# Alpha turned on TensorE, a third half-tile buffer, shared weight scales and a new issue table

## The chip, the cores and the metric

The kernel runs on one core of a Trainium2 chip, in one launch. The metric is the device time of that core in microseconds. One execution was recorded by the hardware profiler; the times on all the tables below are microseconds from the start of that recording unless marked ns.

## The reference

Attention with a learned relative bias, followed by a two-layer feed-forward part. Batch 4, 8 heads, sequence 576, head size 64; 2,304 tokens of width 512, hidden width 2,048.

```python
scores = q @ k.T / 8
x = log1p(abs(i - j)) / log1p(max(i, 1))        # one number per (i, j)
bias = relu(x * w1 + b1) @ w2                   # 32 hidden values -> 8 heads
attn = softmax(scores + bias) @ v               # all in float32
h = attn_rows @ w_in                            # 2304 x 512 @ 512 x 2048
g = max(h, 0) + alpha * min(h, 0)               # alpha: one per hidden column
out = g @ w_out                                 # 2304 x 2048 @ 2048 x 512
```

The two weight matrices arrive as 64-bit floats and are taken apart on the chip with integer operations.

## The kernel before

The kernel keeps near-full precision by splitting most operands into two 16-bit halves, a high and a low one, and adding three matmuls of them. To split a tensor it needs its largest absolute value: one reduction over the columns, a transposition on TensorE, a reduction of the row, a matmul that spreads the result over all partitions (`allmax`, L453 to L461), and four small VectorE operations that make a power of two of it (`p2`, L443 to L452).

The stages are these.
- **Constants and alpha** (L410 to L442). A table of logarithms `cst` is loaded and scaled in place on VectorE by values made of w1 and b1 (L426, L427). `alpha` is loaded by L420 as a 128 x 16 tile, one number at a time. Two half-tile buffers `a16` are cleared at L409.
- **Bias tiles** (`bias_tile`, 36 of them). Each takes four rectified rows from the table on ScalarE (L479), VectorE (L476) or GpSimd (L482), multiplies them by w2 on TensorE (L497), takes the result out of PSUM (L507, L508) and writes it to a scratch area in DRAM, from which the attention units read it back skewed.
- **Weights** (`weights`, L651 to L699), eight blocks of 256 hidden columns. Each block is loaded, put together from 64-bit floats on VectorE (L667, L670), its maxima of w_in and w_out are taken (L674 to L678), the scales made, and the two halves written (high on ScalarE or GpSimd, L691, L692, L697, L698; low on VectorE, L386).
- **q, k and v** (`qk_turn`, `v_rows`). Rows are loaded and turned on TensorE (L577); for v only the maximum is needed (L391, through `absmax`) and, for batches 1 to 3, the halves (L629, L630).
- **Attention units** (`unit`), 8 per batch. Scores (L602 or L603), bias added with the row minimum of the negated sum (L799), exponential (L802), reciprocal of the row sum (L805, L807). For batch 0 the rows are normalised (L822, L823), turned on TensorE (L831) and multiplied with v (L860). For batches 1 to 3 they are normalised into two 16-bit halves in an `a16` buffer (L812 or L813 for the high half, L815 for the low one), turned by a transposing DMA (L818) and multiplied with v by L852. The result goes as halves into a chunk of x (L878, L880).
- **MLP chunks** (`chunk`, `layer_pair`), nine of 256 tokens. For each weight block: first layer L930, activation L937 and L938, halves L941 to L943, second layer L949, output L911, L912, L915.

The order is not left to a scheduler. Every operation has a number, in the order in which the program creates it, and three tables fix the rest: ISSUE lists all 2,806 numbers in the order of issue (a suffix such as .1 picks the second of the engines that may do it), SLOT gives each buffer its place, and IDLE puts dummy matmuls (L997) ahead of certain operations on TensorE: 118 in all. Each engine executes its own operations in the order of the table, waiting where an input is missing; all transfers but a few at the start are issued on SP's queue.

Of the kernel before, what the change touches and what calls it, by code (L numbers as in the profile page):

```python
# [9 lines left out]
F32 = mybir.dt.float32  # L10
# [9 lines left out]
P = 128  # L20
# [122 lines left out]
"""  # L143
IDLE = """
20:11 115:2 52:6 73:2 108:1 35:5 59:3 680:3 94:2 213:2 189:5 45:5 66:1 244:1 631:3 947:2 949:2 652:2 129:1 624:3 687:2 150:2 136:2 708:4 715:2 505:1
694:3 701:5 511:1 743:1 729:5 376:3 542:3 573:7 761:1 775:1 411:2 796:7 786:2 818:2
"""

# [901 lines left out]
```

## Time and profile before

| | us |
|---|---|
| median of 3 runs | 705.16 |
| lowest and highest | 702.3, 707.93 |
| the profiled execution | 702.73 |
| its span | 700.9 |
| TensorE busy | 667.7 (95%) |
| VectorE busy | 498.4 (71%) |
| ScalarE busy | 402.7 (57%) |
| GpSimd busy | 174.7 (25%) |

The span goes from the first to the last instruction that the profiler saw; 1.83 us of the profiled execution lie around it. PE is TensorE, DVE VectorE, ACT ScalarE, POOL GpSimd, SP SyncE; PEld is TensorE's weight load, which overlaps its matmuls. "Busy" counts the time in which the engine executes something; a busy share over the whole span mixes stages with different limits. TensorE's granted clock was full (0.999 on the mean).

### The profile page before, as it was taken

How to read it: one execution, taken by the hardware profiler on the slowest of the kernel's cores; microseconds unless marked ns; L12 is line 12 of the kernel's file. 1: busy time of each engine (PE TensorE's matmuls, PEld its weight loads, DVE VectorE, ACT ScalarE, POOL GpSimd, SP SyncE). 2: the span in 40 equal slices, each digit the busy share in tenths (PEclk: the TensorE clock that was granted, in tenths of full speed). 3: DMA queues.
4: the chain of work that ended last, by engine and by line, in shares of the span. 5: the costliest groups of instructions: out<-in, count | busy, mean ns of one | idle time of the engine just before them, and what ended most of it. 6: DMA issues, size and time to landing. Idle time of an engine off the chain costs nothing.

```text
span 700.9 us, 15311 instructions
## 1 busy us (share of the span) xinstructions
PE 667.7 (95%) x5739; PEld 423.2 (60%) x5739; DVE 498.4 (71%) x1227; ACT 402.7 (57%) x822; POOL 174.7 (25%) x233
## 2 busy tenths in 40 slices
PE   7898899989999999999999999999999999999997
PEld 3454445556656566665667666667566567666664
DVE  5899999997788698987866866677667555232422
ACT  4788999877765575644656465555645352122212
POOL 2555123342113123132322321210221311101010
PEclk9999999999999999999999999999999999999999
DMA  8999899777589799999999979897969963200100
GB/s 199 276 287 340 308 297 297 250 191 189 152 186 182 182 201 221 187 207 220 217 212 179 190 170 205 157 212 172 230 134 196 182 149 62 38 31 1 45 1 31
DMA packets 236374, 125.89 MB, mean 180 GB/s; under 512 B 204684, under 2 KB 204684, under 8 KB 236300
## 3 DMA queue, kind: packets, MB, share of 16 engines
q1 hardware_dynamic: 236168, 124.91, 76.5%
q8 instruction: 45, 0.74, 0.4%
q14 instruction: 29, 0.24, 0.1%
q10 hardware_dynamic: 132, 0.00, 0.0%
HBM read 73.88 MB, written 15.61 MB: 128 GB/s over the span
## 4 chain that ended last, share of the span: by engine, by line
PE 67%; DVE 10%; ACT 9%; DMA 7%; issue 4%; POOL 1%; ACTq 0%; SPq 0%; DVEq 0%; POOLq 0%
PE H L930 24%; PE O L949 22%; PE S L603 5%; PE A L852 5%; DMA at<-a 4%; DVE fg L799 2%; PE S L497 2%; PE S L577 2%; ACT fg L507 2%; PE O L497 2%; ACT at L479 2%; DVE a L815 2%; DMA x<-in_moe_w_out_dram 1%; ACT fg L802 1%; PE A L860 1%
## 5 line engine op out<-in xcount | busy, mean ns | idle before, releaser
L930 PE MATMUL H<-x,win 128*128 128x256 f16 x1728 | 200.7, 273 | 1.5 <-DVE mg L938 1.5
L949 PE MATMUL O<-wout,mg 128*128 128x512 f16 x864 | 197.3, 379 | 1.1 <-DVE mg L915 0.7
L930 PEld LDWEIGHTS <-win 128*128 128x128 f16 x1728 | 166.3, 98 | 34.1 <-issue 8.3
L937 ACT ACTIVATE mg<-H,sm 128x256 f32<-128x256 f32 x144 | 63.6, 469 | 136.8 <-PE H L930 121.1
L949 PEld LDWEIGHTS <-mg 128*128 128x128 f16 x864 | 83.0, 98 | 93.1 <-issue 3.3
L938 DVE SCALAR_TENSOR_TENSOR mg<-H,sm,mg 128x256 f32<-128x256 f32 x144 | 65.4, 478 | 97.8 <-ACT mg L937 97.8
L802 ACT ACTIVATE fg<-fg,st 128x576 f32<-128x576 f32 x144 | 110.5, 768 | 32.3 <-DVE st L799 28.8
L815 DVE SCALAR_TENSOR_TENSOR a<-fg,st,a 128x576 f16<-128x576 f32 x108 | 91.8, 853 | 35.8 <-POOL a L812 17.7
L799 DVE CUSTOM_DVE_ANT_0 fg<-S,fg 128x576 f32<-128x576 f32 x127 | 93.6, 749 | 14.8 <-PE S L603 11.1
L812 POOL TENSOR_SCALAR a<-fg,st 128x576 f16<-128x576 f32 x59 | 47.7, 808 | 179.1 <-DMA at<-a 114.5
L943 POOL TENSOR_TENSOR mg<-mg 128x512 f16<-128x512 f32 x37 | 46.2, 1252 | 120.0 <-DVE mg L941 54.4
L603 PE MATMUL S<-qk 64*128 64x288 f16 (+1 forms) x684 | 55.0, 284 | 5.0 <-DVE qk L584 2.9
L852 PE MATMUL A<-at,five 128*64 128x256 f16 (+3 forms) x720 | 51.5, 288 | 0.6 <-DVE x L880 0.6
L603 PEld LDWEIGHTS <-qk 64*128 64x128 f16 (+1 forms) x720 | 34.2, 96 | 24.7 <-issue 19.1
L813 ACT ACTIVATE a<-fg,st 128x576 f16<-128x576 f32 x49 | 37.6, 770 | 17.3 <-DMA at<-a 15.3
L852 PEld LDWEIGHTS <-five 128*64 128x64 f16 (+1 forms) x720 | 36.1, 109 | 15.2 <-issue 12.0
L805 POOL TENSOR_SCALAR st<-st 128x2 f32<-128x2 f32 (+1 forms) x41 | 12.7, 309 | 105.2 <-ACT fg L802 101.4
L497 PE MATMUL S<-at,w2b 128*32 128x79 f32 (+38 forms) x432 | 34.2, 334 | 4.7 <-ACT fg L507 2.0
L482 POOL TENSOR_SCALAR at<-cst,npsi 128x320 f32<-128x320 f32 (+14 forms) x34 | 27.7, 819 | 44.2 <-PE S L497 25.6
L479 ACT ACTIVATE at<-cst 128x528 f32<-128x528 f32 (+16 forms) x51 | 32.6, 665 | 10.4 <-DVE cst L426 4.2
L997 PE MATMUL H<-sm 128*128 128x512 f16 x118 | 34.8, 406 | 0.9 <-DVE sm L413 0.9
L941 ACT ACTIVATE mg<-mg 128x512 f16<-128x512 f32 x36 | 22.6, 627 | 22.7 <-DVE mg L938 16.6
(150 smaller groups left out, 856.4 us busy)
## 6 DMA issues: line engine op xcount, KB each, us to landing
fg<-scr SPq DMA_DIRECT2D x64, 576.0 KB, 4.7
scr<-fg SPq DMA_DIRECT2D x36, 295.5 KB, 5.1
x<-in_moe_w_out_dram SPq DMA_DIRECT2D x13, 512.0 KB, 5.2
fg<-scr SPq DMA_DIRECT2D x32, 144.0 KB, 3.4
out_dram<-mg SPq DMA_DIRECT2D x18, 256.0 KB, 2.7
five<-in_q_dram SPq DMA_DIRECT2D x32, 128.0 KB, 3.8
mg<-in_moe_w_in_dram SPq DMA_DIRECT2D x8, 512.0 KB, 5.7
x<-in_moe_w_in_dram SPq DMA_DIRECT2D x8, 512.0 KB, 5.5
```

The source lines that it names most:

```text
L479: nc.scalar.activation(hb.t[:, 0:wd], R[:, 0:wd], AF.Relu, bias=PSI[:, g:g + 1], scale=1.0)
L497: nc.tensor.matmul(ps.t[32 * gl:32 * gl + 32, c:n], lhsT=w2b, rhs=x, start=True, stop=True)
L603: return [(lambda a, dst=dst, zq=zq, zk=zk, i=i: nc.tensor.matmul(dst(a), lhsT=tr16(qt)[at, 0, pr, zq, lo:lo + n], rhs=tr16(qt)[at, 1, pr, ...
L799: V(lambda x=x, sl=sl, st=st, ls=ls: nc.vector.tensor_tensor_reduce(out=in_halves(ls[x]()), in0=halves(sl[x].t), in1=in_halves(ls[x]()), s ...
L802: A(lambda x=x, st=st, ls=ls: nc.scalar.activation(ls[x](), ls[x](), AF.Exp, bias=st.t[:, x:x + 1], scale=-1.0, accum_out=st.t[:, 2 + x:3 ...
L812: pl.op([("POOL", 775, lambda x=x, rec=rec, ls=ls, a16=a16: nc.gpsimd.tensor_scalar(a16.t[:, 0:S], ls[x](), rec(), 1.0, op0=ALU.mult, op1= ...
L815: V(lambda x=x, rec=rec, ls=ls, a16=a16: nc.vector.scalar_tensor_tensor(a16.t[:, 640:640 + S], ls[x](), rec(), a16.t[:, 0:S], op0=ALU.mult ...
L852: nc.tensor.matmul(ps.t[64 * hh:64 * hh + 64, 0:w], lhsT=v5[0:hi, zv, n, 2 * pr + hh, :], rhs=at16(at)[0:hi, 5 * za + n, 320 * hh:320 * hh ...
L930: nc.tensor.matmul(hb.t[:, f, :], lhsT=win[:, fp, zw, kb, P * f:P * f + P], rhs=x[:, zx, kb, :], start=(n == 0), stop=(n == 11))
L937: A(lambda f=f: nc.scalar.activation(gf(f), hb.t[:, f, :], AF.Copy, scale=cu[:, f:f + 1]), 470, ky, [hb, t_sig], [(g, f)])
L938: V(lambda f=f: nc.vector.scalar_tensor_tensor(gf(f), hb.t[:, f, :], cs[:, f:f + 1], gf(f), op0=ALU.mult, op1=ALU.max), 475, ky, [hb, t_si ...
L949: nc.tensor.matmul(ob.t[:, t, :], lhsT=gg.t[:, zg, f, P * t:P * t + P], rhs=wout[:, fp, zw, f, :], start=(first and f == 0 and (zg, zw) == ...
```

## The change

Alpha is loaded as 16 rows of 128 numbers, turned by TensorE into PSUM and copied out by VectorE; the transposition is the first operation in TensorE's order, behind twelve dummies. The two `a16` buffers are cleared behind the batch-0 attention units instead of at the start, and a third one lies over the first 640 columns of the constants, cleared when the last bias tile has read them. The weight blocks 0 and 1, and 2 and 3, share one `allmax` and one `p2` of four columns. The maximum of v of batch 0 may go to ScalarE. ISSUE, SLOT and IDLE are replaced throughout: 2,793 operations, 112 dummy matmuls in 39 places.

```diff
-694:3 701:5 511:1 743:1 729:5 376:3 542:3 573:7 761:1 775:1 411:2 796:7 786:2 818:2
+678:2 685:6 727:2 713:2 506:3 706:2 526:5 741:3 557:2 327:1 395:1 780:1 802:5
...
     c_a16 = slots("a16", 2, [P, 1280], F16)
+    c_a16.tiles.append(cstt[:, 0:640].bitcast(F16))
+    c_a16.units.append({("a16", 2)})
...
-    t_gap = [["gap"] for _ in range(2)]
-    for a in range(2):
-        V(lambda a=a: nc.vector.memset(c_a16.tiles[a], 0.0), 700, KEY0 + 900, w=[t_gap[a]])
+    t_gap = [["gap"] for _ in range(3)]
...
-    DMA(lambda e: e.dma_start(out=al, in_=alpha.rearrange("(c p) -> p c", p=P)), 8192, KEY0 + 500, w=[t_al], act_q=True)
+    alr = sb.tile([P, P], F32, name="alr")
+    t_alr = ["alr"]
+    DMA(lambda e: e.dma_start(out=alr[0:16], in_=alpha.rearrange("(c p) -> c p", p=P)), 0, KEY0 + 500, w=[t_alr], act_q=True)
+    aps = Buf(cA)
+    PE(lambda: nc.tensor.transpose(aps.t[:, 0:16], alr[0:16], EYE[0:16, 0:16]), 270, KEY0 + 500, [t_alr, t_c], [aps])
+    V(lambda: nc.vector.tensor_copy(al, aps.t[:, 0:16]), SMALL, KEY0 + 500, [aps], [t_al])
...
-    w_tok = [["w", i] for i in range(NFP)]
+    W_PAIR = 4
+    w_tok = [["w", i - i % 2 if i < W_PAIR else i] for i in range(NFP)]
+    for i in range(0, W_PAIR, 2):
+        w_tok[i + 1] = w_tok[i]
...
-            absmax(mx[:, hf:hf + 1], s, key, [s], [(tok, hf)])
+            alts = [("DVE", 1476, lambda hf=hf, s=s: nc.vector.tensor_reduce(mx[:, hf:hf + 1], s.t, AX.X, ALU.max, apply_absolute_value=True))]
+            if b == 0:
+                alts.append(("ACT", 1450, lambda hf=hf, s=s: nc.scalar.activation(c_a16.tiles[hf], s.t, AF.Abs, accum_out=mx[:, hf:hf + 1])))
+            pl.op(alts, key, [s], [(tok, hf)] + ([t_gap[hf]] if b == 0 else []), tag="mv")
...
-        ar = allmax(m, 2, key, tok)
-        p, ip, s = p2(ar, 2, 2.0 ** -30, key, tok)
...
+        w_late[fp] = (a, bb, va, vb)
+        if fp < W_PAIR and fp % 2 == 0:
+            return
+        fps = [fp - 1, fp] if fp < W_PAIR else [fp]
+        nw = 2 * len(fps)
+        ar = allmax(w_mx[:, 2 * fps[0]:2 * fps[0] + nw], nw, key, tok)
+        p, ip, s = p2(ar, nw, 2.0 ** -30, key, tok)
...
+        for n, fp in enumerate(fps):
+            halves_of(fp, 2 * n, s, tok, key)
...
+    pl.begin("gap", KEY0)
+    for a in range(2):
+        V(lambda a=a: nc.vector.memset(c_a16.tiles[a], 0.0), 700, KEY0 + 900, w=[t_gap[a]])
+    V(lambda: nc.vector.memset(c_a16.tiles[2], 0.0), 700, KEY0 + 900, w=[t_gap[2], t_R, t_T])
     for b in range(1, B):
```

`halves_of` holds the splitting that stood at the end of `weights`, unchanged but for the column of the scales. What the new tables do shows in their first rows, here by engine, as the operation and its part of the program. SP: the constants, w2, alpha, two pieces of weight block 0, then nine of the ten pieces of q and k of batch 0 in a row (before: the constants, b1, a piece of q, w2, alpha, and then q, k and weight pieces mixed). ScalarE: the transfers of b1 and w1, then rectified rows; the warming exponential (L414), which was its first computation, stands behind 21 operations. VectorE: the copy of alpha and alpha's maximum stand ahead of the scaling of the table (L426). At the very end one of the last two output halves is taken out by VectorE and one by ScalarE (before: both by ScalarE).

## Rows read from the trace of the kernel before

**Rows 1.** Busy time by stretch: start:end, length, then busy us of each engine.

```profile
0.00:164.43 164.43, 146.75 (x1442) 78.25 (x1443) 147.40 (x369) 136.97 (x242) 61.21 (x86) 1.00 0.90 269
164.43:250.00 85.57, 82.69 (x668) 54.51 (x668) 68.76 (x190) 54.98 (x116) 19.68 (x31) 1.00 0.78 173
250.00:400.00 150.00, 144.16 (x1255) 95.69 (x1254) 119.64 (x292) 87.41 (x189) 44.06 (x59) 1.00 1.04 208
400.00:560.00 160.00, 158.19 (x1386) 103.95 (x1386) 110.64 (x265) 86.53 (x196) 33.71 (x43) 1.00 0.89 182
560.00:690.00 130.00, 130.00 (x969) 88.23 (x969) 49.96 (x109) 34.68 (x77) 16.04 (x16) 1.00 0.21 47
```

The busy columns are PE, PEld, DVE, ACT and POOL, each with its number of instructions; then PE's granted clock, the busy share of the DMA engines and GB/s.

**Rows 2.** The chain that ended last: start, us, what (first L930).

```profile
164.43 2.73 PE H L930 x24
```

**Rows 3.** Busy time by stretch, up to the first L930; columns as in rows 1.

```profile
0.00:20.00 20.00, 16.29 (x141) 7.16 (x141) 11.24 (x29) 9.33 (x15) 5.42 (x12) 1.00 0.88 215
20.00:60.00 40.00, 35.76 (x441) 19.38 (x439) 37.77 (x79) 32.76 (x55) 21.64 (x28) 1.00 1.02 286
60.00:130.00 70.00, 63.44 (x657) 33.72 (x656) 67.83 (x167) 68.57 (x121) 22.89 (x31) 1.00 0.93 310
130.00:164.43 34.43, 31.27 (x209) 18.00 (x208) 30.56 (x97) 26.30 (x55) 11.26 (x17) 1.00 0.72 196
```

**Rows 4.** Groups by line: busy us, mean ns of one | idle before, releasers.

```profile
L997 PE MATMUL H<-sm 128*128 128x512 f16 x118 | 34.8, 406 | 0.9 <-DVE sm L413 0.9
...
L448 DVE TENSOR_SCALAR sm<-A 128x2 f32<-128x2 f32 (+1 forms) x13 | 2.0, 152 | 0.0
L459 DVE TENSOR_REDUCE sm<-A 2x1 f32<-2x128 f32 (+1 forms) x19 | 5.2, 274 | 2.5 <-PE A L458 2.3
L391 DVE TENSOR_REDUCE sm<-five 128x1 f32<-128x1280 f32 x8 | 11.7, 1475 | 0.0
L409 DVE MEMSET a<- 128x640 uint32 x2 | 1.2, 592 | 0.2
L476 DVE TENSOR_SCALAR at<-cst 128x560 f32<-128x560 f32 (+11 forms) x21 | 10.9, 525 | 3.7 <-PE S L497 3.4 <-PE O L497 0.2
L823 DVE TENSOR_SCALAR fg<-fg,st 128x576 f32<-128x576 f32 x10 | 5.3, 527 | 0.1
L546 ACT ACTIVATE qk<-five 128x1280 f16<-128x1280 f32 x9 | 11.4, 1263 | 1.5 <-DVE sm L735 1.5
L479 ACT ACTIVATE at<-cst 128x528 f32<-128x528 f32 (+16 forms) x51 | 32.6, 665 | 10.4 <-DVE cst L426 4.2 <-PE O L497 3.5 <-PE S L497 2.6
L691 ACT ACTIVATE wout<-wout,sm 128x512 f16<-128x512 f32 x6 | 4.3, 713 | 0.0
```

**Rows 5.** Instructions in order of time, the first 8 us: start, us, engine, line.

```profile
1.18 0.73 SPq L417 DMA_DIRECT2D sm<-in_b_dram  x1
...
1.90 1.28 ACT L414 ACT_TABLE_LOAD   x1 [1.90 <-issue]
...
3.08 0.47 SPq L420 DMA_DIRECT2D sm<-in_moe_alpha_dram  x1
...
3.59 2.98 SPq L524 DMA_DIRECT2D five<-in_q_dram  x1
...
6.18 0.16 DVE L425 TENSOR_TENSOR sm<-sm 128x1 f32<-128x1 f32 x1 [0.65 <-DMA sm<-in_b_dram]
...
7.01 0.52 DVE L426 TENSOR_SCALAR cst<-cst,sm 128x576 f32<-128x576 f32 x1
```

**Rows 6.** Who waited for whom: engine, line, cause: us in total, times, longest.

```profile
POOL a L812 <- DMA at<-a: 114.5, 35, 12.6
...
ACT a L813 <- DMA at<-a: 15.3, 16, 3.0
...
PE A L852 <- DVE x L880: 0.6, 1, 0.6
```

**Rows 7.** Instructions in order of time, the end, on ScalarE.

```profile
696.33 1.27 ACT L911 ACTIVATE mg<-O,sm 128x512 f32<-128x512 f32 x2 [4.81 <-PE O L949]
```

More of the change, by code (lines that the diff above doesn't have):

```diff
@@ L34 @@
 ISSUE = """
[91 rows of a table removed]
[91 rows of a table added]
 """
 SLOT = """
[15 rows of a table removed]
[15 rows of a table added]
 """
 IDLE = """
-20:11 115:2 52:6 73:2 108:1 35:5 59:3 680:3 94:2 213:2 189:5 45:5 66:1 244:1 631:3 947:2 949:2 652:2 129:1 624:3 687:2 150:2 136:2 708:4 715:2 505:1
-694:3 701:5 511:1 743:1 729:5 376:3 542:3 573:7 761:1 775:1 411:2 796:7 786:2 818:2
+7:12 442:1 444:2 73:6 115:3 108:2 52:5 80:2 59:2 664:1 94:4 170:3 45:2 87:1 629:1 122:5 650:2 622:1 636:1 129:1 671:5 481:3 643:3 136:2 692:3 699:4
+678:2 685:6 727:2 713:2 506:3 706:2 526:5 741:3 557:2 327:1 395:1 780:1 802:5
 """
@@ L635, in attention_then_moe @@
     w_mx = cols(16)
-    w_s = {}
+    w_s, w_late = {}, {}
     class Region:
@@ L675, in weights @@
                ("ACT", 1245, lambda: nc.scalar.activation(win[:, fp, 1].rearrange("p a b -> p (a b)"), a.t[:, 0:1024], AF.Abs, accum_out=m[:, 0:1]))],
-              key, [a], [(tok, 0), wreg[fp, 0]], tag="wi")
+              key, [a], [(tok, (fp, 0)), wreg[fp, 0]], tag="wi")
         A(lambda: nc.scalar.activation(wout[:, fp, 1].rearrange("p a b -> p (a b)"), bb.t[:, 0:1024], AF.Abs, accum_out=m[:, 1:2]),
-          1245, key, [bb], [(tok, 1), wreg[fp, 1]])
-        ar = allmax(m, 2, key, tok)
@@ L680, in weights @@
-        p, ip, s = p2(ar, 2, 2.0 ** -30, key, tok)
-        V(lambda: nc.vector.tensor_tensor(pr[:, fp:fp + 1], p[:, 0:1], p[:, 1:2], op=ALU.mult), SMALL, key, [tok], [(t_pr, fp)], cont=True)
-        for i, x, vw, dst in ((0, a, va, lambda z: win[:, fp, z]), (1, bb, vb, lambda z: wout[:, fp, z])):
-            sp = s[:, i:i + 1]
-            ht = ["wh", fp, i]
-            w_s[fp, i] = ht
-            if i:
-                so = cols(2)
-                V(lambda so=so, sp=sp: nc.vector.tensor_scalar(so, sgn[:, 2 * fp:2 * fp + 2], sp, None, op0=ALU.mult), SMALL, key, [tok, t_nal], [(tok, 2)], cont=True)
-                for f in range(2):
-                    sf = so[:, f:f + 1]
-                    on_act = lambda f=f, vw=vw, dst=dst, sf=sf: nc.scalar.activation(dst(0)[:, f], vw()[:, f], AF.Copy, scale=sf)
-                    on_pool = lambda f=f, vw=vw, dst=dst, sf=sf: nc.gpsimd.tensor_scalar(dst(0)[:, f], vw()[:, f], sf, 1.0, op0=ALU.mult, op1=ALU.mult)
-                    pl.op([("ACT", 700, on_act), ("POOL", 690, on_pool)], key, [x, tok], [(ht, (0, f)), wreg[fp, i]], tag="wh")
-                    LO(lambda dst=dst, f=f: dst(1)[:, f], lambda vw=vw, f=f: vw()[:, f], lambda sf=sf: sf, lambda dst=dst, f=f: dst(0)[:, f], 512, key,
-                       [x, tok, (ht, (0, f))], [(ht, (1, f)), wreg[fp, i]])
-                continue
-            on_act = lambda x=x, vw=vw, dst=dst, sp=sp: nc.scalar.activation(dst(0), vw(), AF.Copy, scale=sp)
-            on_pool = lambda vw=vw, dst=dst, sp=sp: nc.gpsimd.tensor_scalar(dst(0), vw(), sp, 1.0, op0=ALU.mult, op1=ALU.mult)
-            pl.op([("ACT", 1137, on_act), ("POOL", 1180, on_pool)], key, [x, tok], [ht, wreg[fp, i]], tag="wh")
-            LO(lambda dst=dst: dst(1), vw, lambda sp=sp: sp, lambda dst=dst: dst(0), 1024, key, [x, tok, ht], [ht, wreg[fp, i]])
@@ new lines, in weights @@
+          1245, key, [bb], [(tok, (fp, 1)), wreg[fp, 1]])
+        w_late[fp] = (a, bb, va, vb)
[5 more added lines that the diff above has]
+        p, ip, s = p2(ar, nw, 2.0 ** -30, key, tok)
+        pairs = p.rearrange("p (n two) -> p n two", two=2)
+        V(lambda: nc.vector.tensor_tensor(pr[:, fps[0]:fps[0] + len(fps)].rearrange("p (n o) -> p n o", o=1), pairs[:, :, 0:1], pairs[:, :, 1:2], op=ALU.mult), SMALL, key, [tok], [(t_pr, z) for z in fps], cont=True)
@@ new lines, in weights, with halves_of @@
+        for n, fp in enumerate(fps):
+            halves_of(fp, 2 * n, s, tok, key)
+    def halves_of(fp, c0, s, tok, key):
+        a, bb, va, vb = w_late[fp]
+        if True:
+            for i, x, vw, dst in ((0, a, va, lambda z: win[:, fp, z]), (1, bb, vb, lambda z: wout[:, fp, z])):
+                sp = s[:, c0 + i:c0 + i + 1]
+                ht = ["wh", fp, i]
+                w_s[fp, i] = ht
+                if i:
+                    so, so_t = cols(2), ["so", fp]
+                    V(lambda so=so, sp=sp: nc.vector.tensor_scalar(so, sgn[:, 2 * fp:2 * fp + 2], sp, None, op0=ALU.mult), SMALL, key, [tok, t_nal], [so_t], cont=True)
+                    for f in range(2):
+                        sf = so[:, f:f + 1]
+                        on_act = lambda f=f, vw=vw, dst=dst, sf=sf: nc.scalar.activation(dst(0)[:, f], vw()[:, f], AF.Copy, scale=sf)
+                        on_pool = lambda f=f, vw=vw, dst=dst, sf=sf: nc.gpsimd.tensor_scalar(dst(0)[:, f], vw()[:, f], sf, 1.0, op0=ALU.mult, op1=ALU.mult)
+                        pl.op([("ACT", 700, on_act), ("POOL", 690, on_pool)], key, [x, tok, so_t], [(ht, (0, f)), wreg[fp, i]], tag="wh")
+                        LO(lambda dst=dst, f=f: dst(1)[:, f], lambda vw=vw, f=f: vw()[:, f], lambda sf=sf: sf, lambda dst=dst, f=f: dst(0)[:, f], 512, key,
+                           [x, tok, so_t, (ht, (0, f))], [(ht, (1, f)), wreg[fp, i]])
+                    continue
+                on_act = lambda x=x, vw=vw, dst=dst, sp=sp: nc.scalar.activation(dst(0), vw(), AF.Copy, scale=sp)
+                on_pool = lambda vw=vw, dst=dst, sp=sp: nc.gpsimd.tensor_scalar(dst(0), vw(), sp, 1.0, op0=ALU.mult, op1=ALU.mult)
+                pl.op([("ACT", 1137, on_act), ("POOL", 1180, on_pool)], key, [x, tok], [ht, wreg[fp, i]], tag="wh")
+                LO(lambda dst=dst: dst(1), vw, lambda sp=sp: sp, lambda dst=dst: dst(0), 1024, key, [x, tok, ht], [ht, wreg[fp, i]])
```

212 rows, old and new, of tables (ISSUE, SLOT) are left out of this document.

## The prediction

> **What bounds the kernel now.** I read the table of busy time by stretch first, then the chain, then the groups, the waits and the start. The table [rows 1] has to be read with one instant in mind, 164.43 us, where the chain shows the first matmul of the MLP's first layer, L930 [rows 2]. From there TensorE is the bound: it is idle for 85.57 - 82.69 = 2.88 us up to 250, 150.00 - 144.16 = 5.84 up to 400, 160.00 - 158.19 = 1.81 up to 560 and not at all from 560 to 690. That is 10.5 us in 525, so after 164.43 a change can win 10.5 us at the most, whatever it does to the other engines.
>
> Before 164.43 nothing on TensorE counts for its own length. It is idle for 17.7 us, and 34.8 of its 146.75 busy us are the 118 dummy matmuls of L997 [rows 4], which only fill waits. VectorE is busy for 147.40 us and ScalarE for 136.97. Split up [rows 3], VectorE is idle for 8.8 us up to 20, then 2.2, 2.2 and 3.9; ScalarE for 10.7, 7.2, 1.4 and 8.1. Between 60 and 130 both are full (67.83 and 68.57 of 70). So the time is: the instant at which these two have put the weights, the bias table and the first attention units behind them, plus TensorE's work from there. The second term hardly changes; the first is what the change works on.
>
> **The change part by part.** I counted, from the two issue tables, which operations have to be issued before the first L930: its inputs, theirs, and all that stands ahead of these on their engines. On VectorE that is 329 operations before and 317 after; on ScalarE 194 and 201; on GpSimd 81 and 82; SP issues 130 and 136 transfers; the dummies are 118 and 112, all of them ahead of it. Durations are those of [rows 4].
>
> VectorE, ahead of the first L930:
> - Two pairs of weight blocks share one maximum and one set of scales. Per pair four small operations and one product (L448 to L451 and L681, each taken at the 0.152 of L448) and one reduction (L459, 0.274) go: 1.03, twice, -2.1 us.
> - One maximum of half of v for batch 0 goes to ScalarE: -1.475 (L391).
> - Two clears at the start (L409, 0.592) go, one of the three new ones lies ahead of L930 (the others come later): -0.6. The copy of the turned alpha: +0.15.
> - Four more bias rows (L476, 0.525): +2.1. Four fewer normalisations (L823, 0.527; GpSimd takes them): -2.1.
> - Six small operations on the scales come earlier, +0.9 at 0.15; five others (three clears, two additions) go, -0.75 at the same price.
>
> Sum: -3.9 us, from 147.4 to 143.5. These durations overlap their neighbours a little, so it is the upper end of what VectorE gains.
>
> ScalarE: the maximum of v (like L546, 1.263), three more bias rows (L479, 0.665 each, 2.0) and two more weight halves (L691, 0.713 each, 1.43): +4.7, from 137.0 to 141.7. GpSimd gives up seven bias rows and a weight half, and takes the four normalisations, three clears and two additions; with 61 us of 164 busy it is not on the path.
>
> So work is moved from the fuller engine to the less full one, and the sum of the two (284.4 us) stays as it is: 285.2. Neither can start before the inputs are there. With the idle time up to 20 us as the part that is not to be had, VectorE could reach 164.43 at 147.4 + 8.8 = 156.2 at the earliest and ScalarE at 137.0 + 10.7 = 147.7; after the change it is 152.3 and 152.4. The floor of the stage falls by 3.8 us. But before, 8.2 us were lost above that floor while ScalarE had room, and now both are full to the same level, so each wait of one for the other is harder to fill. If VectorE alone decides, I get -3.9; if ScalarE decides (1.4 us idle of 70 between 60 and 130), +4.7; if the sum of both does, nothing. I take **-2.0**, half of the floor's fall.
>
> A rule of the Trainium skill speaks against one detail. The row first: ScalarE loads a function table once, 1.28 us, at 1.90 us, while it has nothing to do until the table is scaled at 7.53 [rows 5], and this one load serves the whole kernel. After the change the warming exponential stands behind some 20 us of ScalarE's other work, and the first function is a rectifier. The page "ScalarE: Activation LUTs" (section "What ACT_TABLE_LOAD costs") gives about 2.66 us, with the drain, for every switch to another set, while its section on table sets says that rectifier, copy and absolute value lie in every set. If the rectifier brings a set without the exponential, a second load falls into ScalarE's full stretch: by the page an estimated 2.7 us less gain. From rows alone it is 0 or 1.28; I take 0, as the one load here does serve both kinds.
>
> Alpha. Before, a transfer of 2,048 single numbers is issued at 3.08, and the next issue on SP's queue takes 2.98 us, where the two rows ahead of it took 0.73 and 0.47 [rows 5]. As 16 rows of 512 bytes this stall of some 2.5 us should go. But in this stretch VectorE waits for b1 [rows 5] and later for TensorE's bias matmuls, not for a load behind that stall. Between nothing and -2.5, I take **-0.5**. The new transposition is the first operation in TensorE's order behind twelve dummies, and its copy stands ahead of the scaling of the table (L426, ended 7.53), for which every bias row waits. Alpha is now issued third on SP, near 1.8; b1 was issued at 1.18 and awaited until 6.18, 5.0 us. Taking as long, it lands at 6.8, and the scaling ends up to 0.8 later (0.6 for the landing and some 0.2 for the transposition and the copy, the rest lying beside other small operations); if it lands by 6.2, as b1 did, the cost is nothing. A clear of 0.6, which stood in that place on VectorE, is gone too: I take 0.
>
> The third half-tile buffer. GpSimd waits 114.5 us for transposing transfers before it may write a half again, ScalarE 15.3 [rows 6]. GpSimd has room. The 15.3 us on ScalarE hold up what is queued behind, the MLP's activations among them. But TensorE itself waits for its attention matmul on these halves (L852) once, 0.6 us, and that for something else [rows 6]. So the buffer is worth between nothing and the 10.5 us of TensorE's idle time after 164.43. I take **-1.5**, near the row of L852. What is late next are the halves of q and k and the row minima, not the transfers. The three clears cost 0.6 each on VectorE near the first L930; the table's readers are all done before the third, so nothing else waits for it.
>
> The end. Both last output halves leave PSUM on ScalarE one after the other, 1.27 us [rows 7]; the new order puts one on VectorE: **-0.6**, or nothing if both still wait for the same matmul.
>
> Removed on TensorE: two small transpositions and four tiny matmuls, and six dummies. All lie ahead of 164.43 among waits: 0.
>
> Sum: -2.0 - 0.5 - 1.5 - 0.6 = -4.6. The profiled execution took 702.73 (span 700.9 and 1.8 around it), which gives 698.1. The median shown is 705.16, 2.4 higher, by the scatter of single runs; on it the forecast is **700.6 us**.
>
> **The rivals.**
> - Larger gain (chance 0.2): VectorE was the only bound, the loads come 2.5 us sooner, and the third buffer lets two thirds of TensorE's 10.5 us of idle time go: -3.9 - 2.5 - 7.0 - 0.6 = -14.0, 691.2. For it: VectorE's 95% between 20 and 130. Against it: TensorE's waits after 164.43 name other causes.
> - No effect (0.2): the work is only exchanged between two full engines and the new order is as tight as the old: only the end gains, 704.6. It is also the case in which buffer and alpha do what they say without anything waiting for them. For it: the unchanged sum of 285 us.
> - Slower (0.15): ScalarE takes VectorE's place as the bound of the first stage. Place: 60 to 130 us. It decides from the point where more than ScalarE's 1.4 us of idle time there is added to it; 4.7 - 0.6 gives 709.3. Against it: 8.1 us of idle time behind 130 and 7.2 ahead of 60 can take some of it.
> - The forecast has 0.45, with 696 to 704 as its own range.
>
> **How the numbers follow.** About 1% (7 us) is what a measurement of this kernel can tell from no change: below 698.1 is faster, above 712.2 slower. Faster: nearly all of the large gain (0.19), a third of the forecast (0.15) and a little of the rest: 0.36. Slower: a third of the slower rival and some of the scatter, 0.07. Same: 0.57. The range reaches from the large gain, 690, to the slower rival, 710.
>
> **What would show it.** Right: the first L930 near 162; ScalarE's and VectorE's busy time up to there within 2 us of each other; no long issue behind alpha's; GpSimd's waits for the transposing transfers clearly below 114.5; TensorE's idle time from there to 560 near 9. Wrong: the first L930 later, with ScalarE full from 60 on and VectorE waiting for it, or a second table load (the slower rival); or TensorE's idle time after it halved (the large gain).

## The result, and the profile after

The median after the change is 709.09 us (20 runs, 706.25 to 712.61), before it 705.03 us (20 runs). The ratio is 1.0059, with a 95% interval from 1.0044 to 1.0075: 4.1 us slower where 4.6 us of gain were forecast. The time lies inside the stated range and below the 1% that was named as what can be told from no change, but the interval leaves no room for a gain. In the changed kernel the lines have moved: first layer L930 is L953, second layer L949 is L972, the halves L812, L813 and L815 are L835, L836 and L838, the scaling of the table L426 is L431. (Experiments 7 and 9 to 15, whose tables are printed anew, count three lines more, L956 for L953; experiments 3 and 8 count two more than the kernel before, L814 for L812.)

The profiled execution took 706.25, with a span of 704.5. The table by stretch of the changed kernel, columns as in [rows 1], cut at its own first MLP matmul:

```profile
0.00:167.20 167.20, 145.21 (x1438) 76.38 (x1438) 144.82 (x357) 140.38 (x250) 63.32 (x89) 0.99 0.89 263
167.20:250.00 82.80, 78.37 (x646) 52.62 (x644) 63.75 (x177) 53.40 (x116) 17.63 (x28) 1.00 0.79 174
250.00:400.00 150.00, 144.63 (x1256) 96.22 (x1254) 119.06 (x289) 87.26 (x189) 36.45 (x49) 1.00 1.03 204
400.00:560.00 160.00, 157.87 (x1383) 104.01 (x1383) 113.14 (x277) 85.54 (x196) 38.21 (x51) 1.00 0.92 190
```

Two losses stand there. The first MLP matmul starts at 167.20, not at 164.43. And behind it TensorE is idle for 82.80 - 78.37 = 4.43, then 5.37, then 2.13 us: 11.9 up to 560, where [rows 1] gave 10.5 for a stretch 2.8 us longer. The third buffer should have lowered that number, and GpSimd does wait less for the transposing transfers (who waited for whom, changed kernel; [rows 6] had 114.5 and 15.3):

```profile
POOL a L835 <- DMA at<-a: 67.8, 17, 12.4
ACT a L836 <- DMA at<-a: 5.3, 6, 1.7
POOL cst L835 <- DMA at<-cst: 3.4, 1, 3.4
```

The start shows a delay ahead of the first loss. Instructions in order of time, changed kernel, first 12 us (compare [rows 5]):

```profile
0.72 1.14 ACTq L417 DMA_DIRECT2D sm<-in_b_dram  x1
1.89 0.55 ACTq L416 DMA_DIRECT2D sm<-in_w_dram  x1
1.99 0.42 SPq L422 DMA_DIRECT2D alr<-in_moe_alpha_dram  x1
2.45 0.42 SPq L673 DMA_DIRECT2D x<-in_moe_w_in_dram  x1
2.92 0.47 SPq L673 DMA_DIRECT2D x<-in_moe_w_out_dram  x1
3.43 7.43 SPq L529 DMA_DIRECT2D five<-in_q_dram  x5
9.50 0.15 DVE L426 TENSOR_REDUCE sm<-sm 128x1 f32<-128x1 f32 x1 [8.64 <-DMA sm<-in_w_dram]
10.68 0.52 DVE L431 TENSOR_SCALAR cst<-cst,sm 128x576 f32<-128x576 f32 x1
```

w1, 0.5 KB, is issued at 1.89 and VectorE waits for it until 9.50, so the table is scaled at 11.20 instead of 7.53: 3.7 us later, before any bias row can start. From there to the first MLP matmul the stage takes 167.20 - 11.20 = 156.0 us, against 164.43 - 7.53 = 156.9 before. In this pair of executions the exchange between VectorE and ScalarE gained 0.9 and the start lost 3.7. One execution of each kernel does not settle such numbers: experiment 3 has the same operations up to the first MLP matmul as the kernel before, and scales its table at 7.45, yet in its profiled execution that matmul starts 2.6 us later. In order of time, TensorE, experiment 3:

```profile
167.05 2.79 PE L932 MATMUL H<-x,win 128*128 128x256 f16 x24
```

So the sizes of the losses are taken from the medians of the experiments.

### The profile page after: what moved, and what is told of

Same layout as the page of the kernel before. It is cut to its first block, busy times and chain, and to the rows that moved or that the text cites. A ratio compares the mean times of both kernels' runs of the same rounds, so it can differ in the third digit from the quotient of the medians.

```text
span 704.5 us, 15254 instructions
## 1 busy us (share of the span) xinstructions
PE 665.5 (94%) x5728; PEld 421.3 (60%) x5728; DVE 495.9 (70%) x1214; ACT 400.5 (57%) x824; POOL 173.9 (25%) x235
## 4 chain that ended last, share of the span: by engine, by line
PE 54%; DVE 5%; DMA 3%; issue 3%; ACT 2%; POOL 1%; SPq 0%; POOLq 0%; DVEq 0%; ACTq 0%
PE H L953 22%; PE O L972 21%; PE A L875 5%; PE S L611 4%; DMA at<-a 3%; PE S L585 1%; ACT fg L825 1%; DVE fg L822 1%; DVE mg L961 1%; DVE a L838 1%; ACT mg L960 1%; POOL a L835 1%; DVE mg L965 0%; DVE cst L838 0%; PE O L611 0%
## 5 line engine op out<-in xcount | busy, mean ns | idle before, releaser
L953 PE MATMUL H<-x,win 128*128 128x256 f16 x1728 | 200.8, 273 | 1.4 <-DVE mg L961 1.2
L972 PE MATMUL O<-wout,mg 128*128 128x512 f16 x864 | 197.9, 379 | 2.5 <-DVE mg L938 1.2
L953 PEld LDWEIGHTS <-win 128*128 128x128 f16 x1728 | 166.8, 98 | 35.9 <-issue 8.1
L972 PEld LDWEIGHTS <-mg 128*128 128x128 f16 x864 | 82.1, 98 | 95.5 <-issue 7.5
L838 DVE SCALAR_TENSOR_TENSOR a<-fg,st,a 128x576 f16<-128x576 f32 x74 | 64.5, 874 | 22.5 <-ACT a L836 11.2
L835 POOL TENSOR_SCALAR a<-fg,st 128x576 f16<-128x576 f32 x42 | 34.2, 816 | 118.0 <-DMA at<-a 67.8
L828 POOL TENSOR_SCALAR st<-st 128x2 f32<-128x2 f32 (+1 forms) x48 | 15.1, 315 | 114.9 <-ACT fg L825 108.7
L502 PE MATMUL S<-at,w2b 128*32 128x79 f32 (+37 forms) x492 | 36.2, 334 | 5.7 <-ACT at L484 2.5
L484 ACT ACTIVATE at<-cst 128x432 f32<-128x432 f32 (+17 forms) x53 | 32.7, 647 | 11.1 <-DVE cst L432 5.7
L845 POOL TENSOR_SCALAR fg<-fg,st 128x576 f32<-128x576 f32 x30 | 24.5, 825 | 35.8 <-PE S L610 13.6
L836 ACT ACTIVATE a<-fg,st 128x576 f16<-128x576 f32 x32 | 24.4, 768 | 12.4 <-DMA at<-a 5.3
L838 DVE SCALAR_TENSOR_TENSOR cst<-fg,st,cst 128x576 f16<-128x576 f32 x34 | 28.1, 827 | 4.3 <-ACT cst L836 4.0
```

What stands on the lines that cost most here:

```text
L502: nc.tensor.matmul(ps.t[32 * gl:32 * gl + 32, c:n], lhsT=w2b, rhs=x, start=True, stop=True)
L835: pl.op([("POOL", 775, lambda x=x, rec=rec, ls=ls, a16=a16: nc.gpsimd.tensor_scalar(a16.t[:, 0:S], ls[x](), rec(), 1.0, op0=ALU.mult, op1= ...
L838: V(lambda x=x, rec=rec, ls=ls, a16=a16: nc.vector.scalar_tensor_tensor(a16.t[:, 640:640 + S], ls[x](), rec(), a16.t[:, 0:S], op0=ALU.mult ...
L953: nc.tensor.matmul(hb.t[:, f, :], lhsT=win[:, fp, zw, kb, P * f:P * f + P], rhs=x[:, zx, kb, :], start=(n == 0), stop=(n == 11))
L972: nc.tensor.matmul(ob.t[:, t, :], lhsT=gg.t[:, zg, f, P * t:P * t + P], rhs=wout[:, fp, zw, f, :], start=(first and f == 0 and (zg, zw) == ...
```

## The experiments

All ratios are to the kernel before, with their 95% intervals. My theory at the outset: the late small transfer at the start, and a new order behind the first MLP matmul that loses what the third buffer gains.

**1. w1 first.** The two small transfers on ScalarE's queue change places (2 is w1, 3 is b1).

```diff
-0 3.1 2.1 9 10 11 13 12 5 4 6
+0 2.1 3.1 9 10 11 13 12 5 4 6
```

> The changed kernel, with w1's transfer issued ahead of b1's on ScalarE's queue (two numbers of the issue table change places). Theory (the start): VectorE waited for w1 until 9.50 us instead of 4.49, and the whole first stage is late by that. Then w1 lands near 5, the table is scaled by 8 instead of 11.2, the first L953 comes near 164 instead of 167.2, and the ratio to the kernel before falls from 1.006 to between 0.999 and 1.002. Rival (the new order packs worse, or ScalarE is the bound): the start has slack behind it, the first L953 stays within 1 us of 167, and the ratio stays above 1.004.

Measured: 1.0061 [1.0039, 1.0083]. A miss. In order of time, w1 first:

```profile
4.47 0.15 DVE L426 TENSOR_REDUCE sm<-sm 128x1 f32<-128x1 f32 x1 [3.61 <-DMA sm<-in_w_dram]
10.27 0.16 DVE L430 TENSOR_TENSOR sm<-sm 128x1 f32<-128x1 f32 x1 [5.26 <-DMA sm<-in_b_dram]
```

Now w1 is there at 4.47 and b1, issued second at 1.90, at 10.27. Which of the two goes first is all one; the second is late.

**2. The kernel before with b1 first.** The same exchange in the old kernel: b1 goes to ScalarE's queue ahead of w1.

```diff
-2 4.1 9 10 7 0 5 11 13
+2 5.1 4.1 9 10 7 0 11 13
```

> The kernel before, with b1's transfer moved from SP's queue to ScalarE's and ahead of w1's, as the changed kernel has it; nothing else changes. Theory (the place on the queue makes w1 late): w1 lands later than 7, the first L930 comes 2 to 4 us later than 164.4, ratio 1.003 to 1.006. Rival (w1 is late in the changed kernel because two weight pieces of 512 KB are issued near it, which here come at 6.6): w1 lands by 6.2, where b1 was awaited anyway, and the ratio is within 0.001 of 1.

Measured: 1.0009 [0.9996, 1.0022]. w1, again issued second (1.91), is awaited until 6.50, not 9.50, and the table is scaled at 8.94. So the second place, with its later issue (1.91 instead of 0.73), makes w1 2.0 us late; the 3 us beyond that come from something else in the changed kernel.

**3. The third buffer alone.** The kernel before, its order untouched; the half tiles take three buffers in turn, and one clear follows the first MLP operation.

```diff
     c_a16 = slots("a16", 2, [P, 1280], F16)
+    c_a16.tiles.append(cstt[:, 0:640].bitcast(F16))
+    c_a16.units.append({("a16", 2)})
```

> The kernel before with the third half-tile buffer alone: one more clear behind the first L930, the buffers taken in turn by three, the same issue order. Theory (TensorE does not wait for these buffers): GpSimd's wait for the transposing transfers falls from 114.5 us to under 70, TensorE's idle time between the first L930 and the end stays within 1.5 us of 10.9, ratio 0.999 to 1.001. Rival (the prediction's term and its larger case): TensorE's idle time falls by 1.5 to 7 us, ratio 0.990 to 0.998.

Measured: 0.9941 [0.9923, 0.9959], 4.1 us faster (0.0059 of 704): the rival of what I expected. Who waited for whom, third buffer alone:

```profile
POOL a L814 <- DMA at<-a: 23.4, 8, 11.5
POOL cst L814 <- DMA at<-cst: 13.2, 4, 6.1
```

GpSimd waits 36.6 us for the transfers, half of the 71.2 in the changed kernel, from the same three buffers. So the buffer brings more than the prediction gave it, and something in the changed kernel takes that away.

**4. w1 first, alpha as single numbers.** Experiment 1 with alpha loaded again as 2,048 single numbers, from the same place in SP's order; the transposition turns a constant instead, with the same instructions.

```diff
-    DMA(lambda e: e.dma_start(out=alr[0:16], in_=alpha.rearrange("(c p) -> c p", p=P)), 0, ...
+    DMA(lambda e: e.dma_start(out=al, in_=alpha.rearrange("(c p) -> p c", p=P)), 8192, ...
```

> As e1_w1_first, with alpha loaded as 2,048 single numbers again; the transposition and the copy stay, on the identity and into an unused place. Theory (alpha's form stalls nothing, since the changed kernel has the long issues behind it all the same): ratio within 0.0015 of that of e1_w1_first. Rival (the prediction: the stall of 2.5 us belongs to the single numbers): the issues behind alpha take 2 to 3 us more in all and the ratio is 0.002 to 0.004 above that of e1_w1_first.

Measured: 1.0023 [1.0010, 1.0036]. The slow form of alpha is the faster one, by 0.4%, which neither expectation had. In order of time, alpha as single numbers:

```profile
2.46 2.57 SPq L673 DMA_DIRECT2D x<-in_moe_w_in_dram  x1
5.07 0.47 SPq L673 DMA_DIRECT2D x<-in_moe_w_out_dram  x1
5.58 4.16 SPq L529 DMA_DIRECT2D five<-in_q_dram  x5
6.33 0.16 DVE L430 TENSOR_TENSOR sm<-sm 128x1 f32<-128x1 f32 x1 [1.38 <-DMA sm<-in_b_dram]
```

The stall behind alpha is back (2.57 us for an issue that took 0.42), and it holds the second 512 KB piece back until 5.07. b1 lands by 6.33. Without the stall both pieces, 1 MB, are issued by 3.4 us, and b1's 0.5 KB is there only at 10.27 (experiment 1), about when that megabyte is. The stall also costs SP nothing in the end: the five pieces of q are issued by 5.58 + 4.16 = 9.74, in the changed kernel by 3.43 + 7.43 = 10.86.

**5. The weight pieces held.** The changed kernel with w1 first; the two weight pieces (193 and 205), and the operations that read them, go behind five pieces of q on SP. Alpha stays as rows.

```diff
-0 3.1 2.1 9 10 11 13 12 5 4 6 193 7 8 441 442 16 14 15 17 19 443 194 205 195 23 ...
+0 2.1 3.1 9 10 11 13 12 5 4 6 7 8 441 442 16 14 15 17 19 443 23 24 25 26 27 193 205 ...
```

> The changed kernel with w1 ahead of b1 on ScalarE's queue, and the two weight pieces of 512 KB held on SP's queue until the first five pieces of q are issued. Theory (the two pieces, issued right behind the small transfers, hold back what of these has not landed): b1 lands by 7 us instead of 10.3, the table is scaled by 8, ratio to the kernel before 1.000 to 1.003. Rival (any second transfer on ScalarE's queue is late, or 640 KB of q do the same as 1 MB of weights): b1 lands after 9 again, ratio above 1.004.

Measured: 1.0013 [0.9993, 1.0033]; first MLP matmul at 163.6. In order of time, pieces held:

```profile
2.46 3.17 SPq L529 DMA_DIRECT2D five<-in_q_dram  x5
6.16 0.37 SPq L673 DMA_DIRECT2D x<-in_moe_w_in_dram  x1
6.24 0.16 DVE L430 TENSOR_TENSOR sm<-sm 128x1 f32<-128x1 f32 x1 [1.25 <-DMA sm<-in_b_dram]
6.84 0.51 DVE L431 TENSOR_SCALAR cst<-cst,sm 128x576 f32<-128x576 f32 x1
```

The table is scaled at 7.35, and 1.0059 - 1.0013 = 0.46%, 3.2 us, come back. This is the price of the late start; with both intervals it is 3.2 us give or take 1.8.

**6. Small transfers ahead of the constants.** The changed kernel with w1 on ScalarE's queue and b1 on SP's, ahead of the constants; the weight pieces stay early.

```diff
-0 3.1 2.1 9 10 11 13 12 5 4 6
+0 2.1 3 5 9 10 11 13 12 4 6
```

> The changed kernel with w1 on ScalarE's queue and b1 on SP's, b1 ahead of the constants; the weight pieces stay where the change put them. Theory: b1 lands by 5, the constants by 6, w2 and alpha are small and lie behind 452 KB only, so the table is scaled by 8 and the ratio is 0.999 to 1.003, like the single numbers of alpha gave (1.0023). Rival (the start has slack, and the rest of the new order is what is slow): the table is scaled by 8, but the ratio stays above 1.004.

Measured: 1.0046 [1.0027, 1.0065]. Both small transfers are there by 6.37, but now the constants, 452 KB issued at 1.54, arrive at 7.57, where they took until 4.47 in the changed kernel. The table is scaled at 9.25, not by 8 as both expectations had it. What came last is alpha. In order of time, TensorE, then VectorE:

```profile
8.02 0.20 PE L424 MATMUL A<-cst,alr 16*128 16x16 f32 x1 [2.16 <-DMA alr<-in_moe_alpha_dram]
8.26 0.17 DVE L425 COPY sm<-A 128x16 f32<-128x16 f32 x1 [1.66 <-PE A L424]
```

TensorE waits for alpha, issued at 2.87, until 8.02, and the copy of the turned alpha stands ahead of the scaling on VectorE: here the new place of the transposition costs time. The ratio is 0.13% below that of the changed kernel, which its interval does not tell from nothing.

**7. The late order of before.** The changed kernel up to the 997th operation of its issue table (about the first MLP matmul), from there the operations in the old kernel's order, with the three buffers in turn. The start is unchanged.

With the order 167 operations go back to their old engines and 381 of the 1,115 buffer places change.

> The changed kernel up to operation 997 of its issue table (a little behind the first matmul of the MLP), its start unchanged, and from there the order of the kernel before, with three half-tile buffers. Theory (the new order behind the first MLP matmul leaves TensorE idle for about 4 us more than the old order with a third buffer does): TensorE's idle time from 200 to 276 us falls from 7 to about 3, ratio 0.998 to 1.002. Rival (only the late start makes the change slower): ratio 1.004 to 1.008.

Measured: 0.9974 [0.9958, 0.9989], 0.85% or 6.0 us below the changed kernel (give or take 1.5), with the first MLP matmul still at 166.9. Busy time by stretch, 165 to 600 us, changed kernel, then the old late order:

```profile
165.00:600.00 435.00, 422.87 (x3625) 280.95 (x3625) 321.17 (x799) 242.17 (x536) 101.17 (x139) 1.00 0.89 184
165.00:600.00 435.00, 426.86 (x3660) 283.75 (x3657) 325.34 (x801) 242.73 (x537) 104.82 (x141) 1.00 0.89 184
```

TensorE is idle for 8.1 us instead of 12.1. This is the largest term, and the prediction had none for it.

**8. Third buffer alone, constants back.** Experiment 3 with b1 issued ahead of the constants on SP.

```diff
-2 4.1 9 10 7 0 5 11 13
+2 4.1 5 7 9 10 0 11 13
```

> The kernel before with the third buffer alone, and b1's transfer ahead of that of the constants on SP's queue. Theory (the start shifts all that follows): the table is scaled near 6.3 instead of 7.5, ratio 0.991 to 0.994. Rival (the start has slack, or the constants now set it): ratio that of the third buffer alone, 0.994 to 0.996.

Measured: 0.9978 [0.9963, 0.9993], 0.37% above experiment 3. Both expectations missed: the table came later, not sooner. The constants are awaited until 7.81 and the table is scaled at 9.03 instead of 7.45. A delay of 1.6 us there costs 2.6 here (give or take 1.6), while in experiment 2 a delay of 1.4 cost 0.6 (give or take 0.9): a late table costs, but whether us for us these runs cannot tell.

**9. Both mends.** Experiments 5 and 7 in one kernel: pieces held, and the old order from the 997th operation on.

> The changed kernel with both mends: at the start w1 first on ScalarE's queue, b1 second, and the two 512 KB weight pieces on SP behind five pieces of q (as in the run with held pieces), and from the first MLP matmul on the operations in the old order with three half-tile buffers in turn. If late start (0.46% by the run with held pieces) and late order (0.85% by the run with the old late order) are two separate losses, they add up: 1.0059 - 0.0046 - 0.0085 = 0.993, some 699 us, first MLP matmul near 163.5, TensorE's waits between 165 and 600 near 8 us. If one of them only hides the other, as an earlier first matmul finds its halves no earlier: 0.997, as in the run with the old late order alone.

Measured: 0.9913 [0.9900, 0.9927], 697.89 us, against 0.993 for two losses that add and 0.997 for one that hides the other. They are two losses. This version beats both kernels. First MLP matmul at 163.0, 155.7 us behind the scaled table.

**10. Buffers in turn.** The changed kernel, order unchanged; each half tile takes the buffer longest out of use (65 entries of SLOT).

> The changed kernel, its order unchanged, but every half tile of the units of batches 1 to 3 takes the buffer that has been out of use for longest (65 entries of the buffer table differ). If the loss behind the first MLP matmul comes from the choice of buffers (a half written into one that is still being turned), GpSimd's waits for the transposing transfers fall from 67.8 to some 30 us as in the runs with the old order, and the ratio falls from 1.006 to 0.998. If it comes from the order itself (VectorE's and ScalarE's operations standing in a different row for TensorE), GpSimd's waits fall but the ratio stays at 1.006 and TensorE still loses some 2 us each in 200 to 225 and in 250 to 276.

Measured: 1.0072 [1.0055, 1.0090]. GpSimd's waits for the transfers fall from 71.2 to 52.7 us, not to the 30 that were expected, and the time does not fall. So the choice of half-tile buffers is not the loss, as far as this run changed it.

**11. Both mends, the maximum of v back on VectorE.** One operation of experiment 9 changes its engine (L627).

```diff
-... 91.2 660 93.2 166.1 219 60
+... 91.2 660 93.2 166 219 60
```

> The kernel with both mends, with the one maximum of v of batch 0 taken back from ScalarE to VectorE (1.48 us more there, 1.3 to 1.5 less on ScalarE). If ScalarE is the bound of the first stage (the slower rival of the prediction): 1 us faster than the kernel with both mends, 0.9915. If VectorE is, 1 us slower, 0.9945. If the two hold one another, as the prediction had it, no difference beyond 0.0015.

Measured: 0.9906 [0.9893, 0.9919], 0.5 us below experiment 9, give or take 1.3. It is not the 1 us slower that VectorE as the only bound would give; 1 us faster, for ScalarE, cannot be told from no difference here.

**12. The old order from the 1,400th operation.** As experiment 7, going over later.

> The changed kernel up to the 1,400th operation of its issue table, the old order from there (the run with the old late order went over at the 997th). If the loss of the new late order lies in the stretch from 167 to about 285 us (where TensorE's busy time in 200 to 225 and 250 to 276 fell by 1.9 us each), this run keeps it: 1.004 to 1.006. If it is spread over the whole of the MLP, or lies behind 285 us, most goes: 0.998 to 1.000.

Measured: 1.0053 [1.0041, 1.0065]. The loss is kept whole, so it lies between 167 and, by the expectation's count, about 285 us.

**13 and 14. Engines against order.** Among those 400 operations 31 stand on another engine in the new table; eight of them are high halves moved from GpSimd to ScalarE. Experiment 13 takes experiment 5 and puts the 31 back on their old engines, in the new order. Experiment 14 takes experiment 9 and puts them on their new engines, in the old order.

> Base: the changed kernel with held weight pieces (1.0013). Its order stays, but the 31 operations among the 997th to 1,400th that stand on another engine than in the old table go back to it (8 high halves from ScalarE to GpSimd, 3 the other way, the others one for one). If the loss between 167 and 285 us comes from ScalarE's having too many halves, the ratio falls to 0.991 to 0.993 and TensorE's busy time in 200 to 300 rises from 91.2 to some 94.5 us. If it comes from the order, the ratio stays at 1.000 to 1.002.

> The complement: the kernel with both mends (0.9913, old order from the 997th operation on), with the same 31 operations put on the engines of the new table. If the engines make the loss: 0.999 to 1.001, TensorE's busy time in 200 to 300 falls from 94.2 to some 91 us. If the order makes it: 0.991 to 0.993.

Measured: 1.0017 [0.9995, 1.0038] for 13 and 0.9915 [0.9893, 0.9937] for 14. Busy time by stretch, 200 to 300 us, old engines in the new order:

```profile
200.00:300.00 100.00, 90.99 (x774) 59.20 (x773) 75.40 (x193) 57.43 (x122) 22.27 (x35) 0.98 0.91 182
```

and new engines in the old order:

```profile
200.00:300.00 100.00, 94.79 (x809) 61.72 (x809) 83.46 (x208) 63.81 (x133) 17.28 (x28) 1.00 1.00 201
```

ScalarE and GpSimd change their load as intended (57.43 and 63.81; 22.27 and 17.28), and the first column, TensorE, does not care: it follows the order, about 91 us busy in the new one and 94 to 95 in the old (94.22 in experiment 9, 95.06 in the kernel before). The loss is the order in which the engines take their operations, not which engine has them. What stays open is how much the buffer places that go with the old order (the 381 of experiment 7) have in it: only those of the half tiles were changed alone (experiment 10).

**15. One eviction later.** What such a place looks like can be read in the changed kernel near 202 us. In order of time, ScalarE, then VectorE, then TensorE:

```profile
201.76 0.69 ACT L934 ACTIVATE mg<-O,sm 128x512 f32<-128x512 f32 x1 [3.35 <-PE O L972]
202.34 0.76 ACT L836 ACTIVATE a<-fg,st 128x576 f16<-128x576 f32 x1
...
205.45 0.68 ACT L864 ACTIVATE at<-S 128x640 f32<-128x640 f32 x1
...
203.14 0.82 DVE L838 SCALAR_TENSOR_TENSOR a<-fg,st,a 128x576 f16<-128x576 f32 x1 [3.74 <-ACT a L836]
...
206.18 0.89 PE L611 MATMUL S<-qk 64*128 64x288 f16 x11 [1.62 <-ACT at L864]
```

ScalarE's next operation is to take an output tile out of PSUM (L934), and it waits 3.35 us until TensorE has finished it. The high half behind it (L836) waits with it, though all it needs is there; VectorE waits 3.74 us for that half; the copy L864 is late too, and TensorE waits 1.62 us for it. Experiment 15 is experiment 5 with this one eviction moved behind the two high halves and what lies between.

> Base: the changed kernel with held weight pieces (1.0013). One instruction moves: the output's eviction on ScalarE (L934) that waits 3.35 us for the second layer's last matmul near 201 us goes behind the two high halves and the two operations that stand behind it. If this one place makes the first of the waits (VectorE 3.74 us for the half, TensorE 1.62 us for ScalarE's copy), TensorE's 1.62 us go and with them some 1.5 to 2 us: 0.9985 to 0.9995. If what is gained is waited for again before 300 us, the ratio stays at 1.0013.

Measured: 0.9995 [0.9978, 1.0012], at the upper edge of what was expected if the place counts. The same matmul in order of time, TensorE, eviction moved:

```profile
200.43 0.91 PE L614 MATMUL S<-qk 64*128 64x288 f16 x12
```

The wait is gone: the twelve matmuls run together, and TensorE is busy 92.75 us of 200 to 300 instead of 91.24. The 1.5 us are there in the trace; the ratio fell by 0.0018 from experiment 5, about 1.3 us, and the two intervals overlap, so by time alone it is not shown. TensorE's other waits of over 1 us in that stretch stayed (in experiment 15 1.57 for VectorE's q and k, 1.23 and 1.10 for two evictions); moving each was not tried. So the order is shown to be the loss, and this place only as one part of it.

## Why the prediction was wrong, step by step

Put together, in us of some 704, with uncertainties (95%) worked out from the intervals of the ratios: third buffer -4.1 ± 1.3 (experiment 3), late start +3.2 ± 1.8 (5), late order +6.0 ± 1.5 (7). That makes +5.1; measured are +4.1 ± 1.1, which leaves -1.0 ± 2.4 for all the rest.

The profiled executions, cut at their own first MLP matmul, say the same of two of the terms. From there to the end of the span, the two with the old order and two buffers (the kernel before, 2) take 536.5 and 535.7 us, the six with the old order and three buffers (3, 7, 8, 9, 11, 14) 532.4 to 533.3, and the seven with the new order throughout (the changed kernel, 1, 4, 5, 6, 10, 13) 537.3 to 541.9. On the mean the buffer is worth -3.3 and the order +6.4. Experiment 15, with its one eviction moved, takes 535.3.

- **"The second term hardly changes" is the step that failed.** The whole new issue table was priced by what it moves ahead of the first MLP matmul; behind it I costed only the buffer. The bound I gave, at most 10.5 us to win, is a bound on gains alone and says nothing on what a new order can lose. TensorE's idle time "near 9" came out as 11.9. The order behind the matmul cost 6 us, more than any term of the sum.
- **The start: mechanism missed.** The sum had 0 for it and 0.8 at the worst, by giving alpha b1's 5.0 us. Alpha was not late (TensorE turned it at 5.33); w1 was, by 5 us, and the table by 3.7. I counted the stall behind alpha as a cost and asked what might come sooner without it, not what would then be under way beside a small transfer that matters. The megabyte stood in the listing of SP's new first rows, in the words "two pieces of weight block 0".
- **Alpha, -0.5:** the next two issues take 0.42 and 0.47, so the stall behind it is gone as forecast; but the five issues after them take 7.43, and the queue is no sooner through. Its measured worth at this place is negative, as 1.0061 against 1.0023 shows.
- **The third buffer, -1.5:** right in sign and mechanism, mis-sized; -4.1 was measured, inside the stated bounds of 0 to -10.5. I took the row nearest to TensorE's own wait for the halves, 0.6 us, but waiting halves delay VectorE's and ScalarE's other operations, and TensorE waits for those under other names. With the third buffer alone, the waits of its score matmuls from 164 to 600 us fell from 1.8 to 0.7 for VectorE's row minima and from 2.9 to 2.1 for VectorE's q and k, and one of 0.9 for ScalarE's q and k went. So what the prediction had called "late next" came sooner with the buffer too.
- **The first stage, -2.0:** about right, as far as it can be told. From the scaled table to the first MLP matmul the thirteen profiled executions with the new first stage take 155.2 to 158.1 us, 156.3 on the mean; the four with the old one (the kernel before, 2, 3, 8) take 156.8 to 159.6, 158.2 on the mean. That is 1.9 less, with ranges that overlap. By time, experiment 9 differs from experiment 3 in the main only ahead of the first MLP matmul, its table is as early (7.29 and 7.45), and it is 0.28% or 2.0 us ± 1.6 faster. So this term seems to have come, and the two losses hid it; that it comes from the exchange between VectorE and ScalarE was not tried alone.
- **The end, -0.6:** nothing. In order of time, the end of the changed kernel:

```profile
697.34 2.55 PE L972 MATMUL O<-wout,mg 128*128 128x512 f16 x11 [0.29 <-DVE mg L965]
699.92 0.75 DVE L935 TENSOR_SCALAR mg<-O,sm 128x512 f32<-128x512 f32 x1 [2.65 <-PE O L972]
700.71 0.69 ACT L934 ACTIVATE mg<-O,sm 128x512 f32<-128x512 f32 x1 [5.53 <-DVE mg L935]
```

ScalarE still starts only when VectorE is done: 0.75 + 0.69 one after the other, where [rows 7] had 1.27 for the pair.

- **The table load: right at 0.** One load, in the groups of the changed kernel:

```profile
L484 ACT ACT_TABLE_LOAD x1 | 1.3, 1283 | 4.5 <-DMA cst<-in_const_dram 4.5
```

With the rectifier as the first function there is still one load, 1.28 us, in a stretch where ScalarE is idle. This agrees with the Trainium skill, "ScalarE: Activation LUTs", section "Table sets: the hidden batching unit": cheap functions are in every set, so a rectifier forces no switch.
- **The slower rival gave 709.3, near the 709.09 measured, for a reason that is not the cause.** It made ScalarE the bound of 60 to 130 us. There ScalarE is busy no longer than before, 67.65 us where [rows 3] has 68.57. Busy time by stretch, changed kernel:

```profile
60.00:130.00 70.00, 61.23 (x652) 31.70 (x646) 67.18 (x150) 67.65 (x121) 27.01 (x34) 1.00 0.93 303
```

And the kernel with both mends has the same division of work in the first stage and is 0.9% faster than before. That the number came out near is luck.

## What to carry to other kernels

A new issue order is a change of its own: cost it on every engine and in every stage, above all where one engine's queue holds an operation that must wait for the bound engine ahead of one that need not. Before a slow issue is removed, list what it holds back and what small transfer, not yet landed, would then share the way with a megabyte. When several edits come together, measure each alone and then what is left: here a gain of 4 us was hidden under two losses of 3 and 6, and keeping the gain without them took 0.9% off the time. And a stage read from one execution of each kernel can mislead by half of what is looked for: here one pair gave 0.9 us for what seventeen executions put at 1.9.

## What was not expected of the hardware

**A 0.5 KB transfer behind a megabyte that was issued later, on another queue.** w1 went out on ScalarE's queue at 1.89, the two 512 KB pieces on SP's at 2.45 and 2.92, and w1 was there only at 9.50. With b1 in w1's place, everything else alike (experiment 1), b1 was there at 10.27; with the second piece at 5.07 (4) at 6.33, with both behind 6.1 (5) at 6.24. The Trainium skill, "DMA: Bandwidth & Descriptors", section "Issuing engines are not separate DMA queues", says that transfers of all issuing engines run on the same 16 engines and interleave; the runs agree, and add that here this meant 3 to 4 us for the small one (w1 at 9.50 against 6.50 in experiment 2, b1 at 10.27 against 6.3).

**TensorE's clock falls after a short idle stretch, and the cost is in the matmuls behind.** The 20 runs of the changed kernel have a mean granted clock between 0.987 and 0.997, 0.9916 on the mean; the kernel before has 0.997 over the 23 runs taken beside experiments 1 to 4, the kernel with both mends 0.999 over six. Of the 20, the five with 0.994 or more took 706.25 to 707.60 us, the eight with 0.990 or less 709.39 to 712.61: a good part of the 4.1 us goes with the clock. How much of the late start and of the late order is the clock's and how much that of the waits themselves was not separated. Busy time by stretch, old order from the 1,400th operation (the column behind GpSimd's is the granted clock):

```profile
8.00:12.00 4.00, 0.42 (x2) 0.26 (x3) 1.43 (x9) 0.00 (x0) 0.00 (x0) 0.70 0.72 191
12.00:16.00 4.00, 3.97 (x10) 1.23 (x8) 3.96 (x14) 2.35 (x4) 0.96 (x1) 0.50 0.87 197
...
220.00:224.00 4.00, 3.09 (x10) 1.41 (x10) 3.77 (x10) 1.41 (x2) 0.00 (x0) 0.65 0.79 147
```

While the late table keeps TensorE idle (0.42 us busy from 8 to 12), the granted clock goes down to 0.50, its lower level of 1.2 GHz, and stays there over the next 4 us. Near 220 us it falls again, after two waits. In order of time, TensorE, the same kernel:

```profile
220.91 2.45 PE L975 MATMUL O<-wout,mg 128*128 128x512 f16 x6 [1.23 <-DVE mg L941]
223.16 3.51 PE L956 MATMUL H<-x,win 128*128 128x256 f16 x24
```

and the same six matmuls in the changed kernel's profiled execution, where the clock was full:

```profile
220.38 1.45 PE L972 MATMUL O<-wout,mg 128*128 128x512 f16 x6 [1.22 <-DVE mg L938]
```

1.00 us more for the six, and 0.73 for the 24 behind them (3.51 against 2.78 in the changed kernel's execution): the fall cost 1.7 us in the work after it, where the wait itself, 1.2 us, is the same in both. The fall does not come in every execution, so part of the loss of the new order shows in the medians and not in the profiled execution, which at 706.25 was the fastest of the 20.
